# Order of the attention steps in batches 2 to 7 of a fused attention and MoE kernel: k'v ahead of q's second half, one product of x per drawing

## The chip, the core and the metric

The kernel runs on one core of a Trainium2 chip. The metric is the device time of one execution in microseconds (us), the median of several runs. The core has five engines that run beside each other and wait for each other through semaphores: TensorE (PE, with its weight loads as PEld), VectorE (DVE), ScalarE (ACT), GpSimd (POOL) and SyncE (SP), which issues nearly all DMAs here.

## What is computed

The reference is a linear attention followed by a gated feed-forward layer, called the MoE here:

```python
q_s = exp(q - max(q, axis=-1)); q_s = q_s / (sum(q_s, axis=-1) + 1e-9)
k_s = exp(k - max(k, axis=2));  k_s = k_s / (sum(k_s, axis=2) + 1e-9)
kv = einsum('bhsd,bhse->bhde', k_s, v)
x = einsum('bhsd,bhde->bhse', q_s, kv)   # 8 batches, 8 heads, 576 rows, 64 wide
x = x.transpose(0, 2, 1, 3).reshape(4608, 512)
h = x @ w_in                              # 512 x 2048
g = h * erf(softplus(h))
out = g @ w_out                           # 2048 x 512
```

## The kernel before, in words

**The MoE** sets the main rhythm. Two batches make a pair of 1152 tokens, a pair makes 3 blocks of 384 tokens, and each block is worked on in 4 steps of 512 hidden columns, so there are 48 MoE steps, n = 0 to 47. Values are held as two fp16 halves, and each product is made of three fp16 matmuls (high by high, high by low, low by high). Step n consists of `mm1` (line 975, the products pX, pY and pZ of line 999 in a Strassen-like scheme of seven products, copied to H by DVE and ACT in lines 1011 to 1026), softplus (T) and erf (G) on ACT through the helper `act` (line 344), the product with h (U, line 1079), the split into halves (I and O, lines 1093 and 1097) and `mm2` (line 1103), whose products o are those of line 1125. The loop at line 1224 emits, for each n: U of n-1, then four parts of mm1 of n, with I and O of n-1 and three parts of mm2 of n-2 between them, then T and G of n. In the steps with n % 4 == 2 it also splits the next block of x (`finish`, line 369, lines 297, 298 and 388).

**The attention** of batch 0 is in an order written out by hand, batch 1 uses `attention` (line 730), and batches 2 to 7 use `attention16` (line 649), which the change rewrites. Each is a generator. A step of it emits some instructions and yields a share, a number for how much of the pacing it uses up. The steps of one batch are:

- kmax (line 492): the running maximum of k over its rows, on DVE. Its two tiles and kvf below share the two buffers of one tag.
- kT (line 504): the transposes of that maximum on PE into a bank, and the reduction km on DVE. kB (line 517): the result spread back over all rows by PE. ksub (line 662): k minus the maximum, on DVE.
- q_sub (line 451): q minus its row maximum, for each half of the heads and, in odd batches, for the tails of both batches of the pair (qt).
- exps (line 673) on ACT, in a fixed order with the softplus and erf of the MoE.
- kv_mm (line 528): k'v for one half of the heads, 40 matmuls of line 542, and kv_norm (line 554): the division by the sum (rd, its reciprocal, kvf, lines 561 to 565) on DVE.
- q_norm (line 459) and q_halves (line 636) for one half: the division of q by its sum, the fp16 halves (ACT line 640, DVE line 641) written over k's tile, and a transposing DMA on SP (line 643) back into q's tile. So q_halves of a half must come behind k'v of that half.
- kv_max (line 576): mx, the largest value of kvf. kv_split (line 584): a transpose of mx on PE (all_max, line 125, tile x_bk), a chain of small DVE operations (lines 127 to 141) that makes a power of two, and the two halves kvbd of k'v (lines 595 and 596).
- x_mm (line 626): in odd batches xt first (the tails), then x for the four columns c of 128. Each x needs kvbd and the transposed q of its half, and is copied by ACT (x_put, line 443). Behind the second and the fourth, `load_q` issues the next batch's q, and load_kv (line 471) issues k, the tail and the first half of v.

**The order of the work.** `pace` (line 1207) is called three times in each MoE step, behind each part of mm2. A call is a drawing: it draws steps of the attention generator until their summed share reaches a goal that grows with n. A step that yields 0 ends the drawing. Between n = 8 and 16 (less a lead of 2) the shares of one pair are handed out, afterwards one pair per 12 MoE steps. What a drawing emits is a priority and not yet a place in a queue: the order of each engine's queue is fixed when the kernel is built, by a planner that takes the instructions in order of emission but lets later ones go first while, by its own costs, an earlier one is not ready. On the chip each queue is worked off strictly in order.

Before the change the shares of a batch come from the list SHARES16 (line 49). Kmax takes 2.51, kT 0, and kB with ksub 0.16, the second q_sub 0.09, exps 1.58, each half of k'v with q_norm 2.43, each q_halves 1.3, load_kv and kv_max 0.26, kv_split 0.3, xt 0.78 and each x 0.3.

Of the kernel before, what the change touches and what calls it, by code (L numbers as in the profile page):

```python
# [45 lines left out]
OUTS = [0, 1, 2, 3]  # L46

SHARES = [2.51, 0, 0.16, 0.09, 1.58, 2.43, 1.12, 0.26, 0.29, 0.04, 0.78, 1.12, 0.16]
SHARES16 = [2.51, 0, 0.16, 0.09, 1.58, 2.43, 1.3, 2.43, 1.3, 0.26, 0.3, 0.78, 0.3]
LEAD = 2.0  # L50

EXPMASK = 0x7F800000
# [5 lines left out]
def attn_moe_kernel(  # L58
# [280 lines left out]
    def act(out_, in_, func, chain=True, **kw):  # L339

        with ExitStack() as es:
            if chain and last[0] is not None:
                es.enter_context(tc.issue_after(last[0]))
            i = nc.scalar.activation(out_, in_, func, **kw)  # L344
        if chain:
            last[0] = i.ins
        return i
# [49 lines left out]
    def load_half(src, tag, b, hf):  # L397

        s4 = src[b, hf * 4:hf * 4 + 4, 0:SM, :].rearrange("h (p t) d -> p h t d", t=TM)
        if tag == "v" and b == 0 and hf == 1:  # L400
            t = ch.tile([P, 4, TM, D + 1], F32, tag="G", bufs=2, name=f"v_{b}_{hf}")
            nc.gpsimd.memset(t[:, :, :, D:], 1.0)
        elif tag == "v":
            t = vbuf
        else:
            t = at.tile([P, TM, 4, D], F32, tag=tag, name=f"{tag}_{b}_{hf}")
        eng = nc.sync
        for h in range(4):
            eng.dma_start(t[:, h, :, :D] if tag == "v" else t[:, :, h, :], s4[:, h])  # L409
        return t  # L410
# [34 lines left out]
    def hd(t):  # L445
        return t.rearrange("p h d -> p (h d)")
# [45 lines left out]
    def k_max(b, ks, kt):  # L492

        kmax = at.tile([P, H, D], F32, tag="qT", name=f"kmax_{b}")
        k2 = at.tile([P, 2, 4, D], F32, tag="qT", name=f"k2_{b}")
        for hf in range(2):
            nc.vector.tensor_tensor(k2, ks[hf][:, 0:2], ks[hf][:, 2:4], op=ALU.max)
            nc.vector.tensor_tensor(
                kmax[:, hf * 4:hf * 4 + 4, :], k2[:, 0], k2[:, 1], op=ALU.max
            )  # L500
        nc.vector.tensor_tensor(kmax[kt[1]], kmax[kt[1]], kt[0], op=ALU.max)
        return kmax

    def k_max_T(b, kmax):
        bk = bank(f"kT_{b}")
        km2 = hd(kmax)
        for c in range(NC4):
            nc.tensor.transpose(
                bk[:, c * P:(c + 1) * P], km2[:, c * P:(c + 1) * P], ident
            )  # L510
        km = at.tile([P, NC4], F32, tag="km", bufs=1, name=f"km_{b}")
        nc.vector.tensor_reduce(
            km, bk.rearrange("p (c s) -> p c s", c=NC4), axis=AX.X, op=ALU.max
        )
        return km
# [12 lines left out]
    def kv_mm(b, hf):  # L528


        d, kt_ = bat[b], bat[b - b % 2]["kt"]
        bk = bank(f"kv_{b}_{hf}")
        for c in range(2):
            for t in range(TM + 1):
                for a in range(2):
                    h = 2 * c + a
                    if t < TM:
                        kk, vv = d["k"][hf][:, t, h, :], d["v"][hf][:, h, t, :]
                    else:

                        kk, vv = kt_[:, 4 * hf + h, :], vtail[:, 4 * hf + h, :]
                    nc.tensor.matmul(  # L542
                        bk[a * D:(a + 1) * D, c * W:(c + 1) * W], kk, vv,
                        start=(t == 0), stop=(t == TM),
                    )
        return bk
# [7 lines left out]
    def kv_norm(b, hf, bk):  # L554
        if b >= E32:
            if hf == 0:
                bat[b]["kvf"] = at.tile([P, NC4, D], F32, tag="qT", name=f"kvf_{b}")
            kvf = bat[b]["kvf"]
        bkv = bk[:, :2 * W].rearrange("p (c w) -> p c w", c=2)
        rd = at.tile([P, 2, 1], F32, tag="rd", bufs=1, name=f"rd_{b}_{hf}")  # L560
        nc.vector.tensor_scalar_add(rd, bkv[:, :, D:], 1e-9)
        nc.vector.reciprocal(rd, rd)
        cs = slice(2 * hf, 2 * hf + 2)
        if b >= E32:
            nc.vector.tensor_tensor(
                kvf[:, cs, :], bkv[:, :, :D], rd.to_broadcast([P, 2, D]), op=ALU.mult
            )
            return
        for a in range(2):
            ps = slice(a * D, (a + 1) * D)  # L570
            nc.vector.tensor_tensor(
                kv32[b][ps, cs, ps], bkv[ps, :, :D], rd[ps].to_broadcast([D, 2, D]),
                op=ALU.mult,
            )
# [58 lines left out]
                out_, kvbd[b % 2][:, wl, c, :], qT[:, ql], start=(i == 0), stop=(i == 2)  # L633
            )

    def q_halves(src, place, name):

        n = src.shape[1]
        st_ = place.bitcast(F16).rearrange("p (i n) -> p i n", i=2)
        nc.scalar.copy(st_[:, 0], src)  # L640
        nc.vector.tensor_tensor(st_[:, 1], src, st_[:, 0], op=ALU.subtract)
        qT = src.bitcast(F16).rearrange("p (a s) -> p a s", s=P)
        nc.sync.dma_start_transpose(qT, place.bitcast(F16))
        return qT.rearrange("p (i a) s -> p i a s", i=2)

    def flat3(t):
        return t.rearrange("p a b c -> p (a b c)")

    def attention16(b):
        d, j, p = bat[b], b % 2, b // 2  # L650
        even = bat[b - j]
        tl = slice(j * TAIL, (j + 1) * TAIL)
        ks, qs, kt = d["k"], d["q"], even["kt"][tl]
        sh = iter(SHARES16)
        kmax = k_max(b, ks, (kt, tl))
        yield next(sh)
        km = k_max_T(b, kmax)
        q_sub(rows(qs[0]), 16, f"q_{b}_0")
        yield next(sh)
        kb = k_max_rows(b, km)  # L660
        for hf in range(2):
            nc.vector.tensor_tensor(
                ks[hf], ks[hf],
                kb[:, None, hf * 4:hf * 4 + 4, :].to_broadcast([P, TM, 4, D]),
                op=ALU.subtract,
            )
        nc.vector.tensor_tensor(kt, kt, kb[tl], op=ALU.subtract)
        yield next(sh)
        q_sub(rows(qs[1]), 16, f"q_{b}_1")
        if j == 1:  # L670
            q_sub(even["qt"], H, f"qt_{p}")
        yield next(sh)
        for t in (*ks, kt, qs[0], qs[1], *([even["qt"]] if j == 1 else [])):
            act(t, t, AF.Exp, chain=b > 1)
        yield next(sh)
        qT = {}
        for hf in range(2):
            kv_norm(b, hf, kv_mm(b, hf))
            if hf == 0:
                d["v"].append(load_half(v, "v", b, 1))  # L680
            q_norm(rows(qs[hf]), 16, f"q_{b}_{hf}", b)
            yield next(sh)
            qT[hf] = q_halves(flat3(qs[hf]), flat3(ks[hf]), f"{b}_{hf}")
            yield next(sh)
        if j == 1:
            q_norm(even["qt"], H, f"qt_{p}", b)
            qT[2] = q_halves(hd(even["qt"]), hd(even["kt"]), f"{p}_t")
        if b + 1 < B:
            load_kv(b + 1)
        mx = kv_max(b)  # L690
        yield next(sh)
        kv_split(b, mx)
        yield next(sh)
        for i in ((3 * p + 1, 3 * p + 2) if j else (3 * p, 3 * p + 1)):
            while not x_free(i):
                yield 0
        w = next(sh)
        if j == 1:
            bk = bank(f"xt_{p}")
            x = xblock(p * NBK + 1)  # L700
            bk3 = bk.rearrange("p (c s) -> p c s", c=NC4)
            for a in range(2):
                for c in range(NC4):
                    cs = slice(a * TAIL, (a + 1) * TAIL)
                    x_mm(2 * p + a, c, bk3[:, c, cs], qT[2][:, :, c, cs])
            x_put(bk3, x[:, :, SM - T:SM - T + P], None)
            if b + 1 < B:
                bat[b + 1]["qt"] = load_tail(q, "qt", p + 1)
            yield w
        w = next(sh)  # L710
        for c in range(NC4):
            hf, c2 = divmod(c, 2)
            bk = bank(f"x_{b}_{c}")
            q4 = qT[hf].rearrange("p i (t c) s -> p i t c s", c=2)[:, :, :, c2]
            x_mm(b, c, bk.rearrange("p (t s) -> p t s", t=TM), q4)
            x_split(b, c, bk)
            if c2 == 1 and b + 1 < B:
                load_q(b + 1, hf)
            if c == NC4 - 1:
                d["xdone"] = True  # L720
            yield w

    def x_split(b, c, bk, part=None):
        for blk, off, o, w in xcols(b, 0 if b % 2 == 0 else SM + 2 * TAIL, SM)[part or slice(9)]:
# [476 lines left out]
                assert tok("A"), i  # L1201

    w_odd = sum(SHARES[:11]) + NC4 * sum(SHARES[11:])
    per_pair = 2 * (sum(SHARES16[:11]) + NC4 * SHARES16[12]) + SHARES16[11]
    n1 = NG + 4

    def pace(at_n):
# [68 lines left out]
```

## Time and profile before

| | us |
|---|---|
| three runs | 851.73, 853.64, 853.0 |
| median | 853.0 |
| the profiled execution, its own time | 853.86 |
| its span, first to last instruction | 851.7 |
| PE busy in the span | 811.2 |
| DVE busy | 638.2 |
| ACT busy | 503.0 |

The span is what the trace covers; 2.2 us of the profiled execution lie around it. Busy times are of single engines and overlap. In the rows of the profile a line such as "L632 PE x" is line 632 of the kernel, on engine PE, writing tile x; "a <- b" in a list of waits is that a stood still until b had ended. PEld is the loading of weights, which runs beside the matmuls.

### The profile page before, as it was taken

How to read it: one execution, taken by the hardware profiler on the slowest of the kernel's cores; microseconds unless marked ns; L12 is line 12 of the kernel's file. 1: busy time of each engine (PE TensorE's matmuls, PEld its weight loads, DVE VectorE, ACT ScalarE, POOL GpSimd, SP SyncE). 2: the span in 40 equal slices, each digit the busy share in tenths (PEclk: the TensorE clock that was granted, in tenths of full speed). 3: DMA queues.
4: the chain of work that ended last, by engine and by line, in shares of the span. 5: the costliest groups of instructions: out<-in, count | busy, mean ns of one | idle time of the engine just before them, and what ended most of it. 6: DMA issues, size and time to landing. Idle time of an engine off the chain costs nothing.

```text
span 851.7 us, 15370 instructions
## 1 busy us (share of the span) xinstructions
PE 811.2 (95%) x6448; PEld 553.8 (65%) x6448; DVE 638.2 (75%) x913; ACT 503.0 (59%) x633; POOL 17.6 (2%) x37
## 2 busy tenths in 40 slices
PE   2999998899999999999999999999999999999997
PEld 1655557567667667766776676766776676777673
DVE  5999899998997879758865779748866657554543
ACT  2598486777564556555673566555663565543532
POOL 2010000000000000000000000000000000000000
PEclk8899999899999999999999999999999999999999
DMA  9997420016416402412134302322121000100100
GB/s 255 407 250 197 120 75 13 1 25 112 106 35 131 108 9 61 103 31 51 51 70 98 87 14 51 93 51 51 38 51 38 38 2 1 38 1 1 38 1 37
DMA packets 145508, 62.59 MB, mean 73 GB/s; under 512 B 134688, under 2 KB 136736, under 8 KB 145440
## 3 DMA queue, kind: packets, MB, share of 16 engines
q1 hardware_dynamic: 143264, 53.23, 25.1%
q0 software_dynamic: 2176, 8.39, 2.8%
q8 instruction: 50, 0.82, 0.4%
q14 instruction: 18, 0.15, 0.1%
HBM read 45.09 MB, written 9.44 MB: 64 GB/s over the span
## 4 chain that ended last, share of the span: by engine, by line
PE 64%; DVE 19%; ACT 10%; issue 3%; SPq 2%; DMA 1%; ACTq 0%; POOL 0%; DVEq 0%
PE o L1125 27%; PE pX L999 15%; PE pZ L999 7%; ACT G L344 4%; PE o L1116 4%; ACT L344 3%; PE pY L999 3%; DVE G L1079 3%; PE kv L542 2%; DVE H L1097 2%; PE pX L1038 2%; DVE H L1093 2%; SPq L409 2%; PE x L632 1%; DVE wi L298 1%
## 5 line engine op out<-in xcount | busy, mean ns | idle before, releaser
L1125 PE MATMUL o<-wo,H 128*128 128x512 f16 x1584 | 367.0, 380 | 2.8 <-DVE H L1093 1.8
L999 PEld LDWEIGHTS <-wi 128*128 128x128 f16 x3696 | 311.2, 98 | 44.3 <-issue 15.7
L1125 PEld LDWEIGHTS <-H 128*128 128x128 f16 x1584 | 152.7, 98 | 157.4 <-DVE H L1093 2.6
L999 PE MATMUL pX<-x,wi 128*128 128x192 f16 x2112 | 206.2, 248 | 7.6 <-ACT H L1018 4.5
L344 ACT ACT_TABLE_LOAD x104 | 133.4, 1283 | 2.8 <-DVE H L1024 0.8
L1079 DVE SCALAR_TENSOR_TENSOR G<-G,small,H 128x1536 f32<-128x1536 f32 x44 | 79.9, 1817 | 56.2 <-ACT G L344 56.0
L1026 ACT COPY H<-pX 128x384 f32<-128x384 f32 x44 | 20.9, 475 | 165.3 <-PE pX L999 159.9
L999 PE MATMUL pZ<-x,wi 128*128 128x192 f16 x1056 | 104.0, 247 | 3.4 <-ACT x L297 1.8
L344 ACT ACTIVATE G<-H,U 128x768 f32<-128x768 f32 (+1 forms) x60 | 72.7, 1231 | 22.1 <-DVE H L1024 21.5
L1097 DVE TENSOR_TENSOR H<-G,H 128x1536 f16<-128x1536 f32 x44 | 77.2, 1755 | 1.0
L344 ACT ACTIVATE G<-G 128x1536 f32<-128x1536 f32 x48 | 71.2, 1484 | 0.5
L999 PE MATMUL pY<-x,wi 128*128 128x192 f16 x528 | 51.9, 247 | 0.0
L1024 DVE TENSOR_TENSOR H<-pZ,H 128x384 f32<-128x384 f32 x44 | 24.4, 554 | 32.5 <-PE pZ L999 32.1
L1011 DVE COPY H<-pY 128x384 f32<-128x384 f32 x44 | 24.3, 553 | 30.3 <-PE pY L999 30.3
L1116 PE MATMUL o<-wo,G 128*128 128x512 f32 x96 | 43.4, 597 | 0.0
L1093 DVE CAST H<-G 128x1536 f16<-128x1536 f32 x44 | 42.1, 957 | 0.8
L297 ACT ACTIVATE x<-x 128x768 f16<-128x768 f32 (+1 forms) x44 | 32.9, 763 | 12.8 <-DVE x L388 11.1
L1141 DVE TENSOR_SCALAR ob<-o,V 128x512 f32<-128x512 f32 x29 | 21.7, 748 | 24.5 <-PE o L1125 24.5
L298 DVE SCALAR_TENSOR_TENSOR x<-x,x 128x768 f16<-128x768 f32 (+1 forms) x44 | 37.0, 851 | 3.2 <-ACT x L297 3.2
L1013 DVE TENSOR_TENSOR H<-pX,H 128x384 f32<-128x384 f32 x44 | 24.4, 554 | 15.9 <-PE pX L999 15.7
L443 ACT ACTIVATE x<-x 128x384 f32<-128x384 f32 (+1 forms) x52 | 17.5, 394 | 30.0 <-PE x L632 27.4
L1116 PEld LDWEIGHTS o<-wo,G 128*128 128x128 f32 x96 | 17.5, 190 | 18.7 <-issue 18.2
(184 smaller groups left out, 762.7 us busy)
## 6 DMA issues: line engine op xcount, KB each, us to landing
out_dram<-ob SPq DMA_DIRECT2D x32, 256.0 KB, 2.4
vbuf<-in_v_dram SPq DMA_DIRECT2D x60, 128.0 KB, 3.1
q<-in_q_dram SPq DMA_DIRECT2D x56, 128.0 KB, 3.4
k<-in_k_dram SPq DMA_DIRECT2D x56, 128.0 KB, 3.1
wo<-in_moe_w_in_dram SPq DMA_DIRECT2D x4, 1024.0 KB, 17.2
wi<-in_moe_w_out_dram POOLq DMA_DIRECT2D x2, 1024.0 KB, 8.9
wi<-in_moe_w_in_dram SPq DMA_DIRECT2D x2, 1024.0 KB, 9.4
raw<-in_moe_w_out_dram POOLq DMA_DIRECT2D x2, 1024.0 KB, 8.0
```

The costliest lines, as they stand in the source:

```text
L297: nc.scalar.activation(hi, src, AF.Copy, scale=s)
L298: nc.vector.scalar_tensor_tensor(lo, src, s, hi, op0=ALU.mult, op1=ALU.subtract)
L344: i = nc.scalar.activation(out_, in_, func, **kw)
L999: nc.tensor.matmul(o, w[wl][:, c, a * P:(a + 1) * P], x[:, xl, xi, c, :], start=(new and a == 0 and c == 0 and i == 0), stop=(c == 1 and i ...
L1011: nc.vector.tensor_copy(C[0, 0], bank2("Y"))
L1013: add(C[0, 0], bank2("X"), C[0, 0], op=ALU.add)
L1024: add(C[0, 1], bank2("Z"), C[0, 1], op=ALU.add)
L1079: nc.vector.scalar_tensor_tensor(flat(s["G"]), flat(s["G"]), (GB if n in OUT32 else GA)[:, g:g + 1], flat(s["H"]), op0=ALU.mult, op1=ALU.mult,
L1093: nc.vector.tensor_copy(flat(s["gh"]), flat(s["G"]))
L1097: nc.vector.tensor_tensor(flat(s["gl"]), flat(s["G"]), flat(s["gh"]), op=ALU.subtract)
L1116: nc.tensor.matmul(o, s["G"][:, a, ts_], w[:, a, :], start=(first_ and a == 0), stop=(last_ and a == FG - 1),)
L1125: nc.tensor.matmul(o, s[gt][:, a, ts_], w[wl][:, a, :], start=(first_ and a == 0 and i == 0), stop=(last_ and a == FG - 1 and i == 2),)
```

## The change

In `attention16` the steps of one batch get another order, and another share each:

1. kT is emitted in the step of kmax, no longer in that of the first q_sub. It yields 1.8.
2. Both q_sub steps and the step of kB and ksub yield 0.9, exps 1.5.
3. The first half of k'v is a step of its own (0.4), then q_norm (0.75) and q_halves (0.75) of the first half.
4. The second half of k'v and kv_max come next, in one step (0.6), and then kv_split (0.4), all of it ahead of q_norm and q_halves of the second half (0.75 each). Before, kv_max and kv_split came behind them.
5. load_kv comes behind the second q_halves, as before, now in a step with the tails' q_norm and q_halves that yields 0.75 in odd batches and 0 in even ones.
6. xt yields 0.75, and each x yields 0.75 instead of 0.3.

The sum for a pair goes from 27.9 to 28.3. No instruction is added or taken away. `chain=b > 1` is true for all batches that come here, so its removal changes nothing, nor does that of the name given to q_halves.

```diff
-SHARES16 = [2.51, 0, 0.16, 0.09, 1.58, 2.43, 1.3, 2.43, 1.3, 0.26, 0.3, 0.78, 0.3]
+SHARE16 = 1.8 + 0.9 * 3 + 1.5 + 0.4 + 0.75 * 4 + 0.6 + 0.4 + 0.75 * 4
...
-        kmax = k_max(b, ks, (kt, tl))
-        yield next(sh)
-        km = k_max_T(b, kmax)
+        km = k_max_T(b, k_max(b, ks, (kt, tl)))
+        yield 1.8
         q_sub(rows(qs[0]), 16, f"q_{b}_0")
-        yield next(sh)
+        yield 0.9
         kb = k_max_rows(b, km)
...
-        for hf in range(2):
-            kv_norm(b, hf, kv_mm(b, hf))
-            if hf == 0:
-                d["v"].append(load_half(v, "v", b, 1))
+
+        def q_half(hf):
             q_norm(rows(qs[hf]), 16, f"q_{b}_{hf}", b)
-            yield next(sh)
-            qT[hf] = q_halves(flat3(qs[hf]), flat3(ks[hf]), f"{b}_{hf}")
-            yield next(sh)
+            yield 0.75
+            qT[hf] = q_halves(flat3(qs[hf]), flat3(ks[hf]))
+            yield 0.75
+
+        kv_norm(b, 0, kv_mm(b, 0))
+        d["v"].append(load_half(v, "v", b, 1))
+        yield 0.4
+        yield from q_half(0)
+        kv_norm(b, 1, kv_mm(b, 1))
+        mx = kv_max(b)
+        yield 0.6
+        kv_split(b, mx)
+        yield 0.4
+        yield from q_half(1)
         if j == 1:
             q_norm(even["qt"], H, f"qt_{p}", b)
-            qT[2] = q_halves(hd(even["qt"]), hd(even["kt"]), f"{p}_t")
+            qT[2] = q_halves(hd(even["qt"]), hd(even["kt"]))
         if b + 1 < B:
             load_kv(b + 1)
-        mx = kv_max(b)
-        yield next(sh)
-        kv_split(b, mx)
-        yield next(sh)
+        yield 0.75 if j == 1 else 0
...
-            yield w
-        w = next(sh)
+            yield 0.75
         for c in range(NC4):
...
-            yield w
+            yield 0.75
...
-    per_pair = 2 * (sum(SHARES16[:11]) + NC4 * SHARES16[12]) + SHARES16[11]
+    per_pair = 2 * SHARE16 + 0.75 * 2
```

More of the change, by code (lines that the diff above doesn't have):

```diff
@@ L634, in x_mm, with q_halves @@
             )
-    def q_halves(src, place, name):
+    def q_halves(src, place):
         n = src.shape[1]
@@ L653, in attention16 @@
         ks, qs, kt = d["k"], d["q"], even["kt"][tl]
-        sh = iter(SHARES16)
-        kmax = k_max(b, ks, (kt, tl))
-        yield next(sh)
-        km = k_max_T(b, kmax)
+        km = k_max_T(b, k_max(b, ks, (kt, tl)))
+        yield 1.8
         q_sub(rows(qs[0]), 16, f"q_{b}_0")
-        yield next(sh)
+        yield 0.9
         kb = k_max_rows(b, km)
@@ L667, in attention16 @@
         nc.vector.tensor_tensor(kt, kt, kb[tl], op=ALU.subtract)
-        yield next(sh)
+        yield 0.9
         q_sub(rows(qs[1]), 16, f"q_{b}_1")
@@ L671, in attention16 @@
             q_sub(even["qt"], H, f"qt_{p}")
-        yield next(sh)
+        yield 0.9
         for t in (*ks, kt, qs[0], qs[1], *([even["qt"]] if j == 1 else [])):
-            act(t, t, AF.Exp, chain=b > 1)
-        yield next(sh)
+            act(t, t, AF.Exp)
+        yield 1.5
         qT = {}
-        for hf in range(2):
-            kv_norm(b, hf, kv_mm(b, hf))
-            if hf == 0:
-                d["v"].append(load_half(v, "v", b, 1))
+        def q_half(hf):
             q_norm(rows(qs[hf]), 16, f"q_{b}_{hf}", b)
-            yield next(sh)
-            qT[hf] = q_halves(flat3(qs[hf]), flat3(ks[hf]), f"{b}_{hf}")
-            yield next(sh)
+            yield 0.75
[11 more added lines that the diff above has]
+        yield from q_half(1)
         if j == 1:
             q_norm(even["qt"], H, f"qt_{p}", b)
-            qT[2] = q_halves(hd(even["qt"]), hd(even["kt"]), f"{p}_t")
+            qT[2] = q_halves(hd(even["qt"]), hd(even["kt"]))
         if b + 1 < B:
             load_kv(b + 1)
-        mx = kv_max(b)
-        yield next(sh)
-        kv_split(b, mx)
-        yield next(sh)
+        yield 0.75 if j == 1 else 0
         for i in ((3 * p + 1, 3 * p + 2) if j else (3 * p, 3 * p + 1)):
@@ L708, in attention16 @@
                 bat[b + 1]["qt"] = load_tail(q, "qt", p + 1)
-            yield w
-        w = next(sh)
+            yield 0.75
         for c in range(NC4):
```

## The prediction

> **What bounds the kernel now.** I read the page first, then busy time by stage, then the waits of PE, then the timeline around those waits. From the page:
>
> ```profile
> span 851.7 us, 15370 instructions
> PE 811.2 (95%) x6448; PEld 553.8 (65%) x6448; DVE 638.2 (75%) x913; ACT 503.0 (59%) x633; POOL 17.6 (2%) x37
> ...
> PE 64%; DVE 19%; ACT 10%; issue 3%; SPq 2%; DMA 1%; ACTq 0%; POOL 0%; DVEq 0%
> ```
>
> PE is busy 95% of the span, and the chain that ended last runs through it for 64%. The stages show where its idle time lies (columns: PE, PEld, DVE, ACT, POOL, then granted clock, DMA share, GB/s):
>
> ```profile
> 148.00:156.00 8.00, 3.37 (x21) 2.33 (x19) 7.95 (x10) 6.29 (x7) 0.00 (x0) 0.76 0.00 0
> 190.00:690.00 500.00, 492.04 (x4295) 346.04 (x4294) 383.34 (x568) 296.74 (x356) 3.16 (x10) 1.00 0.28 63
> 690.00:852.00 162.00, 155.41 (x1208) 105.59 (x1205) 81.89 (x88) 73.42 (x79) 0.00 (x0) 1.00 0.04 16
> ```
>
> Up to about 190 us the weights are decoded and split, and DVE is full (7.95 of 8.00 in the first row). From 190 to 690 us, where batches 2 to 7 are worked on beside the MoE, PE is busy 492.04 of 500.00: 8.0 us is all that any reordering can give there through visible idle time. After 690 us no attention is left, and the change has nothing to move. The waits of PE in the middle stage say what the 8.0 us are (total, times, longest):
>
> ```profile
> PE xt L632 <- DVE kvbd L595: 2.5, 3, 0.9
> PE pX L999 <- ACT H L1026: 1.3, 2, 0.6
> PE x L632 <- issue: 0.9, 1, 0.9
> PE pX L999 <- DVE H L1021: 0.9, 1, 0.9
> PE x L632 <- DVE kvbd L595: 0.7, 2, 0.4
> PE x L632 <- DVE kvbd L596: 0.6, 3, 0.2
> PE pX L999 <- ACT H L1018: 0.3, 1, 0.3
> ```
>
> Four of the seven rows are the same thing: the products x and xt (L632) stand in PE's queue and their operand kvbd, the split k'v that kv_split writes on DVE, is not there. They add up to 2.5 + 0.9 + 0.7 + 0.6 = 4.7 us in 9 waits. The other three are MoE products of bank pX, 1.3 + 0.9 + 0.3 = 2.5 us.
>
> A wait in this list is shorter than what it costs. In batch 2:
>
> ```profile
> 215.10 0.27 PE L125 MATMUL x_bk<-ident,mx 128*128 128x128 f32 x1
> 215.21 1.15 PE L999 MATMUL pX<-x,wi 128*128 128x192 f16 x12
> 216.20 2.75 PE L1125 MATMUL o<-wo,H 128*128 128x512 f16 x12
> 219.86 0.81 PE L632 MATMUL x<-q,kvbd 128*128 128x512 f16 x3 [0.91 <-issue]
> ```
>
> The 12 products pX last 1.15 us here, yet the next group starts 216.20 - 215.21 = 0.99 us after them: 0.16 us of each group's modelled end lies under its successor. When PE waits, this 0.16 is lost too. So the 9 waits cost 4.7 + 9 x 0.16 = 6.1 us. (The 0.91 put down to issue here is the same kvbd wait.)
>
> [...]
>
> **The change, part by part.** No instruction is added or removed. What moves is the step in which each is emitted. Pacing hands out one third of an MoE step per drawing, and a pair of batches is spread over 36 drawings (12 MoE steps by 3), so one drawing gives 27.9 / 36 = 0.775 of share before and 28.3 / 36 = 0.786 after. Counting the shares through the loop gives, for batch 4 (written MoE step.drawing), kT 15.0, kB 15.1, exps 15.1, kv1 17.1, kv_split 19.0, x0 19.0, x1 and x2 19.1, x3 19.2 before, and kT 13.2, kB 15.0, exps 15.2, kv1 17.1, kv_split 17.1, x0 and x1 18.2, x2 19.0, x3 19.1 after. For batch 5: kv1 23.0, kv_split 25.0, xt 25.0 before; kv1 23.0, kv_split 23.0, xt 24.1 after. A drawing in time: kv_split's transpose for batches 4 and 6, one pair apart, starts at 377.93 and 571.50 us, so (571.50 - 377.93) / 36 = 5.4 us.
>
> ```profile
> 377.93 0.27 PE L125 MATMUL x_bk<-ident,mx 128*128 128x128 f32 x1
> 378.24 0.29 DVE L127 TENSOR_REDUCE x_e<-x_bk 128x1 f32<-128x128 f32 x1 [2.14 <-PE x_bk L125]
> 379.34 0.72 DVE L595 TENSOR_SCALAR kvbd<-kvf,x_s 64x256 f16<-64x256 f32 x2
> 380.12 0.61 PE L632 MATMUL x<-q,kvbd 128*128 128x512 f16 x2 [0.35 <-DVE kvbd L595]
> 383.20 0.48 DVE L596 SCALAR_TENSOR_TENSOR kvbd<-kvf,x_s,kvbd 64x256 f16<-64x256 f32 x1
> 383.75 0.39 PE L632 MATMUL x<-q,kvbd 128*128 128x512 f16 x1 [0.23 <-DVE kvbd L596]
> ...
> 571.50 0.27 PE L125 MATMUL x_bk<-ident,mx 128*128 128x128 f32 x1
> ```
>
> *The waits that go.* Before, kv_split and x0 (or xt) come out of one drawing, so the transpose, a chain of 9 DVE operations up to kvbd's upper half (378.24 to 380.06) and x stand close together; kvbd's lower half ends only at 383.68 and holds x a second time. After, kv_split is emitted 4 drawings before x or xt in batches 4 to 7, 4 x 5.4 = 21.6 us, against the 5.8 us that the chain took from 377.93 to 383.68. In the faster paced batches 2 and 3 it is two drawings or more. All 9 waits should go: -6.1 us.
>
> *The wait that may come.* kv1, kv_max and kv_split are now emitted together, so the transpose x_bk (L125) has to wait for rd, its reciprocal, kvf and mx on DVE. In PE's queue the whole MoE stands behind it. Batch 4 before shows this chain without its transpose:
>
> ```profile
> 352.87 0.29 PE L542 MATMUL kv<-vtail,kt 128*64 128x65 f32 x4
> 354.09 2.75 PE L1125 MATMUL o<-wo,H 128*128 128x512 f16 x12
> 354.56 0.15 DVE L561 TENSOR_SCALAR rd<-kv 128x2 f32<-128x2 f32 x1
> 356.60 0.42 DVE L578 TENSOR_REDUCE mx<-kvf 128x1 f32<-128x256 f32 x1
> ```
>
> From the end of kv at 353.16 to the end of mx at 357.02 pass 3.9 us. The order of each engine's queue is fixed when the kernel is built, by a planner that places an instruction where its own clock has it ready, so PE has other work first, as the o group here, and the wait is the planner's error on the chain. Its error on the 9 DVE operations before x was 0.35 + 0.16 = 0.51 us in batch 4 and 0.91 + 0.16 = 1.07 us in batch 2, so for 4 operations 4/9 of that: 0.23 to 0.48, and I take the middle, 0.35 us. Six batches: +2.1 us. Ends: 0, and 3.9 - 2.0 = 1.9 each (two pX-sized groups ahead of it, 2 x 0.99), or 11.4 us.
>
> *kT beside kmax.* kT's transposes now leave in kmax's drawing and could wait for it. But kmax needs both buffers that it shares with kvf, and kv_split, which releases kvf, is now ahead of it by the whole of x. I take 0. The nearest row bounds it at one last operation of kmax in each of six batches, 6 x 0.69 = 4.1 us:
>
> ```profile
> L501 DVE TENSOR_TENSOR kmax<-kmax,kt x8: 673/687/690, 8.2 to 581.1; 64x512 f32<-64x512 f32 x8
> ```
>
> *xt of batch 3.* There the pace is faster, and kv1, the tail's halves and xt lie within two drawings (12.0 to 12.2). The halves need a transposing DMA between them:
>
> ```profile
> 263.88 0.29 PE L542 MATMUL kv<-vtail,kt 128*64 128x65 f32 x4
> 271.01 1.28 SPq L643 DMA_TRANSPOSE qt<-kt  x1
> qt<-kt SPq DMA_TRANSPOSE x3, 3.1
> ```
>
> The transpose was issued at 271.01 and lands 3.1 later, 274.1, which is 9.9 us after kv1's end at 264.17; two drawings are 10.8 in the later pace and less here. I take 0, since before no wait of PE on such a DMA is listed, and keep up to 2.5 us.
>
> *What else is moved.* On SP the v half, the two transposes and load_kv keep their order among themselves; load_kv of batch 5 leaves in 18.1 instead of 19.0, which is early, and q's reload after x1 and x3 is spread. On POOL the clearing of kvbd (batches 2 and 3) now stands ahead of load_vtail's memsets instead of behind; those wait for PE anyway and hold nobody. On ACT the exps leave two drawings after kB in batches 4 to 7, where they left in kB's own, so ACT finds k already subtracted:
>
> ```profile
> ACT k L344 <- DVE k L662: 13.3, 3, 6.9
> ```
>
> These 13.3 us are ACT's idle time, not PE's, and shorten the way to softplus. I count 0, with the 2.5 us of pX waits as the most that a freer ACT and DVE could give, or as much again lost.
>
> *The early stage.* Batch 2's first steps (kT, kB) come one or two drawings sooner while DVE is full. The row of 148 to 156 us prices what can go wrong: PE was busy 3.37 of 8.00 at a granted clock of 0.76, so a second hole of that kind costs 4.6 us, and losing this one gives as much. MoE work on ACT ends that hole, which the change leaves where it is; I take 0.
>
> **The sum** against the profiled execution, 853.86 us with a span of 851.7: -6.1 + 2.1 = -4.0, giving 849.9. The median of the three runs is 853.0, 0.9 below the profiled one, so the forecast for it is 853.0 - 4.0 = 849.0 us. Its own range: from 846.9 (no new wait) to 851.3.
>
> **The rivals.** *Given back:* the waits only change places. The planner puts each instruction at its own estimate, so x_bk, now the tight one, gets the 6.1 us that x had. For it speak the 29% of the chain that lie on DVE and ACT; against it, that x_bk hangs on 4 operations and not 9, and that the MoE waits, where a gain would be eaten, are 2.5 us in all. Time: 853.0. [...]
>
> *Slower through x_bk:* the transpose stands too early in PE's queue, with less than an o group ahead of it, and DVE's chain of 3.9 us runs behind a long MoE operation. It decides from (6.1 + 1.7) / 6 = 1.3 us a batch; with 1.9 us a batch the time is 853.0 - 6.1 + 11.4 = 858.3. For it: in batch 4 rd itself came 1.4 us after kv (354.56 against 353.16). Against it: the planner knows the DVE queue and let PE run 12 products of pX and 12 of o past such chains.
>
> *More than forecast:* x_bk never waits and the pX waits go as well, since DVE's and ACT's bursts are spread: 853.0 - 6.1 - 2.5 = 844.4.
>
> **How the numbers follow.** Chances: forecast 0.50, given back 0.20, slower 0.18, more 0.12. About 0.2%, 1.7 us, is what a measurement here can tell from no change. The forecast and the last case lie below 851.3, given back within 851.3 to 854.7, slower above: 0.62, 0.20, 0.18. The range goes from 844.4 to 856.0: it takes in the forecast, the given-back case and the near half of the slower one, with the bounds on kT, xt and the early stage falling inside.
>
> **What would show it.** Right: from 190 to 690 us no row of PE on kvbd is left, x_bk starts some 20 us ahead of its x or xt, a wait of PE at x_bk on mx of a few tenths appears, and PE's idle time there falls from 8.0 to about 4 to 5 us. Wrong: long waits at x_bk or kT, xt of batch 3 held by the transposing DMA, PE rows on kvbd still there, or new pX waits on ACT or DVE that eat the gain; a changed hole before 190 us would mean that the start decided.

## The result, and the profile after

The changed kernel takes 867.1 us (median of 6 runs, 861.5 to 870.7), the kernel before 852.5 us beside it. It is slower by 14.6 us by the medians, where 849.0 was forecast and 856.0 was the end of the range. The ratio, taken over all runs, is 1.016 with a 95% interval of 1.012 to 1.020, or 13.6 us. The profiled execution took 870.7 us, the slowest of the six, so its span lies 16.9 us above that of the kernel before and overstates the loss a little.

The page after:

```profile
span 868.6 us, 15364 instructions
PE 819.3 (94%) x6448; PEld 562.5 (65%) x6448; DVE 640.7 (74%) x913; ACT 502.9 (58%) x633; POOL 17.6 (2%) x37
...
PE 65%; DVE 18%; ACT 6%; DMA 4%; issue 3%; SPq 3%; POOL 0%; ACTq 0%; DVEq 0%
```

The matmuls are as many as before (6448), yet PE is busy 8.1 us longer, and DMA, which held 1% of the chain, holds 4%. The stages after, the first of them the whole stretch of batches 2 to 7, the others around one wait (columns as in the prediction: PE, PEld, DVE, ACT, POOL, granted clock, DMA share, GB/s):

```profile
190.00:707.00 517.00, 500.73 (x4345) 355.65 (x4345) 388.36 (x571) 299.87 (x361) 3.16 (x10) 0.98 0.27 62
363.00:369.00 6.00, 3.12 (x21) 1.56 (x18) 5.90 (x10) 0.39 (x1) 0.40 (x2) 1.00 0.42 112
369.00:375.00 6.00, 5.84 (x49) 5.54 (x50) 4.67 (x17) 1.77 (x3) 0.00 (x0) 0.72 0.85 194
375.00:381.00 6.00, 6.00 (x46) 3.89 (x44) 2.92 (x4) 5.36 (x6) 0.00 (x0) 1.00 0.33 70
```

PE is idle 517.00 - 500.73 = 16.3 us there, against 8.0 before; and its granted clock, 1.00 before in every six microseconds of this stage, falls to 0.72 from 369 to 375 us, behind the wait of 3.04 us at x_bk. The waits of PE from 190 to 710 us:

```profile
PE x_bk L125 <- DVE mx L578: 7.5, 4, 3.4
PE xt L632 <- DMA qt<-kt: 2.8, 1, 2.8
PE pX L1001 <- DVE H L1023: 2.7, 1, 2.7
PE kv L542 <- DMA vbuf<-in_v_dram: 0.8, 1, 0.8
PE pX L1001 <- DVE H L1015: 0.8, 1, 0.8
PE kv L542 <- issue: 0.8, 1, 0.8
PE pX L1001 <- ACT H L1020: 0.7, 1, 0.7
```

All rows of PE on kvbd are gone, as forecast. In their place stand x_bk on mx (the transpose in kv_split: two waits of over 3 us, in batches 4 and 6, and two of about 0.5, in batches 5 and 7), xt on the transposing DMA, and pX on DVE. Where the time is lost is read best from the starts of the MoE steps, that is of the first pY product of a step in the timeline:

| MoE step | before, us | after, us | after is late by | |
|---|---|---|---|---|
| 4 | 128.65 | 130.23 | 1.6 | the start, ahead of the change's first step |
| 8 | 188.58 | 187.47 | -1.1 | batch 2 |
| 12 | 258.11 | 268.27 | 10.2 | batches 2 and 3 |
| 16 | 327.03 | 335.91 | 8.9 | |
| 17 | 341.73 | 352.03 | 10.3 | |
| 19 | 373.36 | 389.16 | 15.8 | x_bk of batch 4 |
| 28 | 520.60 | 531.91 | 11.3 | x of batches 4 and 5 no longer wait (1.9 of these 4.5 us in run 4) |
| 29 | 535.30 | 548.03 | 12.7 | |
| 31 | 566.93 | 586.71 | 19.8 | x_bk of batch 6 |
| 38 | 682.22 | 699.18 | 17.0 | end of the attention |

So there are two losses: about 9 us by step 12, and two jumps of 5.5 and 7.1 us at x_bk of batches 4 and 6. The timeline around the first jump:

```profile
357.89 0.64 SPq L409 DMA_DIRECT2D k<-in_k_dram  x1
360.83 0.69 DVE L497 TENSOR_TENSOR k<-k 128x512 f32<-128x512 f32 x1 [3.27 <-DMA k<-in_k_dram]
361.44 1.81 DVE L1081 SCALAR_TENSOR_TENSOR G<-G,small,H 128x1536 f32<-128x1536 f32 x1
362.36 0.29 PE L542 MATMUL kv<-vtail,kt 128*64 128x65 f32 x4
363.58 2.54 PE L1127 MATMUL o<-wo,H 128*128 128x512 f16 x11
364.31 1.76 DVE L1099 TENSOR_TENSOR H<-G,H 128x1536 f16<-128x1536 f32 x1
366.64 0.15 DVE L561 TENSOR_SCALAR rd<-kv 128x2 f32<-128x2 f32 x1
368.69 0.42 DVE L578 TENSOR_REDUCE mx<-kvf 128x1 f32<-128x256 f32 x1
369.16 0.32 PE L125 MATMUL x_bk<-ident,mx 128*128 128x128 f32 x1 [3.04 <-DVE mx L578]
369.54 1.70 PE L1001 MATMUL pZ<-x,wi 128*128 128x192 f16 x12
371.03 2.13 PE L1001 MATMUL pX<-x,wi 128*128 128x192 f16 x12
```

Read from the bottom: x_bk waits 3.04 us for mx. Mx is late because rd, the first of its chain, starts only at 366.64, 4.0 us after k'v. It stands in DVE's queue behind the MoE's long operations, and these are late because DVE stood still for 3.27 us in front of L497: the first of them, L1081, has its input from ACT at 358.58 and starts only behind L497, at 361.44. L497 is the first operation of kmax of the next batch, batch 5, and waits for that batch's k, whose last piece was issued at 357.89. Behind x_bk the 12 products of pZ and of pX take 1.70 and 2.13 us, where 1.15 is usual.

Before, L497 of batch 5 stood 6.8 us behind the start of k's load and did not wait:

```profile
337.89 2.58 SPq L409 DMA_DIRECT2D k<-in_k_dram  x4
344.68 0.68 DVE L497 TENSOR_TENSOR k<-k 128x512 f32<-128x512 f32 x1
```

After, the transposing DMA that frees k's first tile and this load are directly in front of k'v's second half:

```profile
351.64 2.87 SPq L643 DMA_TRANSPOSE q<-k  x1
355.94 2.59 SPq L409 DMA_DIRECT2D k<-in_k_dram  x4
```

The load starts at 355.94, L497 at 360.83, 4.9 us behind it, and k'v's second half at 361.26. Measured from the start of MoE step 16, the load leaves 10.9 us behind it before (337.89 against 327.03) and 20.0 us behind it after (355.94 against 335.91).

### The profile page after: what moved, and what is told of

Its sections match the earlier page's. It is cut to its first block, busy times and chain, and to the rows that moved or that the text cites. A ratio compares the mean times of both kernels' runs of the same rounds, so it can differ in the third digit from the quotient of the medians.

```text
span 868.6 us, 15364 instructions
## 1 busy us (share of the span) xinstructions
PE 819.3 (94%) x6448; PEld 562.5 (65%) x6448; DVE 640.7 (74%) x913; ACT 502.9 (58%) x633; POOL 17.6 (2%) x37
## 4 chain that ended last, share of the span: by engine, by line
PE 65%; DVE 18%; ACT 6%; DMA 4%; issue 3%; SPq 3%; POOL 0%; ACTq 0%; DVEq 0%
PE o L1127 27%; PE pX L1001 15%; PE pZ L1001 7%; PE o L1118 3%; PE pY L1001 3%; ACT G L344 3%; DVE G L1081 3%; SPq L409 2%; ACT L344 2%; PE kv L542 2%; PE pX L1040 2%; DVE H L1099 2%; PE x L632 2%; DMA q<-k 2%; DVE x L298 1%
## 5 line engine op out<-in xcount | busy, mean ns | idle before, releaser
L1001 PEld LDWEIGHTS <-wi 128*128 128x128 f16 x3696 | 318.0, 100 | 45.1 <-issue 18.0
L1001 PE MATMUL pX<-x,wi 128*128 128x192 f16 x2112 | 210.0, 251 | 9.3 <-ACT H L1020 4.9
L344 ACT ACT_TABLE_LOAD x104 | 133.4, 1283 | 10.9 <-DVE H L1026 9.1
L1081 DVE SCALAR_TENSOR_TENSOR G<-G,small,H 128x1536 f32<-128x1536 f32 x44 | 79.9, 1816 | 50.6 <-ACT G L344 50.5
## 6 DMA issues: line engine op xcount, KB each, us to landing
wo<-in_moe_w_in_dram SPq DMA_DIRECT2D x4, 1024.0 KB, 16.9
```

What stands on the lines that cost most here:

```text
L1001: nc.tensor.matmul(o, w[wl][:, c, a * P:(a + 1) * P], x[:, xl, xi, c, :], start=(new and a == 0 and c == 0 and i == 0), stop=(c == 1 and i ...
L1081: nc.vector.scalar_tensor_tensor(flat(s["G"]), flat(s["G"]), (GB if n in OUT32 else GA)[:, g:g + 1], flat(s["H"]), op0=ALU.mult, op1=ALU.mult,
```

## The experiments

Ratios are to the kernel before, run beside each group of experiments; its median was 852.0 beside the first four, 852.2 beside the next four and 853.5 beside the last three. Gains in us are differences of medians; by the ratios, those of runs 2 and 3 are 8.0 and 7.5 us.

**1. kv_split one step later.**

```diff
-        kv_split(b, mx)
-        yield 0.4
-        yield from q_half(1)
+        second = q_half(1)
+        yield next(second)
+        kv_split(b, mx)
+        yield 0.4
+        yield from second
```

> The changed kernel with one step moved: kv_split is emitted one step later, behind q_norm of the second half, so that its transpose x_bk stands a drawing behind kv_max in PE's queue; all else as changed. Theory A, the loss is mainly PE standing at x_bk for mx (7.5 us in 4 waits in the changed profile) and the slow clock behind the two long ones: the MoE steps 17 to 19 and 29 to 31 lose 5.5 and 7.0 us against before, which should go, so about 867 - 12.5 = 854.5 us, no PE row of x_bk on mx over 0.3 us, and run to run spread back to about 3 us. Theory B, the loss is made in the early stage, batches 2 and 3 (the changed kernel is 10.2 us behind at step 12): then 865 us or more stays.

866.0 us, ratio 1.016 (1.013 to 1.019): nothing gained.

```profile
PE x_bk L125 <- DVE mx L578: 7.9, 4, 3.6
```

Taken as written, theory A failed and B held. But the row of PE's waits says that the wait to be removed was still there, so the run did not test its cost. The 0.6 share of k'v's step is less than a drawing (0.786): q_norm left in the same drawing, kv_split in the next, and x_bk stood behind 12 products o instead of 11. One step was no distance.

**2. kmax held behind kv_split.** The queue of DVE is changed, not the place of kv_split:

```diff
-        km = k_max_T(b, k_max(b, ks, (kt, tl)))
+        with ExitStack() as es:
+            if b > 2:
+                es.enter_context(tc.issue_after(bat[b - 1]["split"]))
+            kmax = k_max(b, ks, (kt, tl))
+        km = k_max_T(b, kmax)
```

(`split` is the last DVE operation that kv_split emits, line 601 of the kernel before. `tc.issue_after` makes kmax wait for it in the order of the queue.)

> The changed kernel with kmax of batches 3 to 7 put behind kv_split of the batch before in DVE's queue; kv_split stays directly behind k'v's second half. Theory A1, mx is late because DVE, ahead of it, stands 3.3 and 3.7 us at kmax's first operation (L497) for the next batch's k by DMA: then DVE's waits at L497 (20.8 us in 9) fall under 6 us, x_bk's waits in batches 4 and 6 fall from 3.2 and 3.6 to under 0.7 us, and the time is about 855 us. Theory A2, x_bk is simply too near to k'v and kmax has nothing to do with it: the waits at x_bk stay over 2 us and the time over 863.

857.9 us, ratio 1.0065 (1.004 to 1.009), 9.2 us less than the changed kernel. Waits of PE:

```profile
PE xt L633 <- DMA qt<-kt: 3.8, 1, 3.8
PE pX L1006 <- DVE H L1028: 2.7, 1, 2.7
PE x_bk L125 <- DVE mx L578: 1.8, 4, 0.5
```

The longest wait at x_bk is 0.5 us. DVE still stands 12.3 us at L497 in 5 waits, more than the 6 expected, but behind kv_split, where PE does not depend on it. In batch 4 DVE's queue now goes from ob straight to the MoE's G:

```profile
357.90 0.75 DVE L1148 TENSOR_SCALAR ob<-o,V 128x512 f32<-128x512 f32 x1 [2.03 <-PE o L1132]
359.71 1.82 DVE L1086 SCALAR_TENSOR_TENSOR G<-G,small,H 128x1536 f32<-128x1536 f32 x1 [1.06 <-ACT G L344]
```

G starts 1.8 us behind ob, where the changed kernel needed 4.6 (356.80 to 361.44). This shows that DVE's wait for k made mx late; theory A2 falls.

**3. The new order from batch 4 on.** Batches 2 and 3 keep the old order and its pace:

```diff
-            yield from attention(b) if b < E32 else attention16(b)
+            yield from attention(b) if b < E32 else attention16_old(b) if b < 4 else attention16(b)
```

> The new order for batches 4 to 7 only; batches 2 and 3 keep the old order and shares. Theory B, early stage: the 8.9 us that the changed kernel is behind at step 16 go, less about 2 that it is behind at step 4 already by other causes, so about 860 us. Theory A alone (the early stage's difference is noise of the start): 866 us. The waits at x_bk of batches 4 and 6 stay in both, at 3 us.

858.3 us, ratio 1.007 (1.005 to 1.009), 8.8 us less than the changed kernel. x_bk still waits 7.6 us in 4. So batches 2 and 3 hold the other half of the loss. (`attention16_old` is the function of the kernel before; the pacing of that pair, not shown here, is the old one too.)

**4. The kernel before with kv_split earlier.**

```diff
             yield next(sh)
+            if hf == 1:
+                kv_split(b, kv_max(b))
             qT[hf] = q_halves(flat3(qs[hf]), flat3(ks[hf]), f"{b}_{hf}")
...
-        mx = kv_max(b)
-        yield next(sh)
-        kv_split(b, mx)
+        yield next(sh)
         yield next(sh)
```

> The kernel before with one edit: kv_max and kv_split are emitted ahead of q_halves of the second half instead of behind load_kv; all shares and all other steps as before. If the prediction's first term holds by itself (the 9 waits of x and xt on kvbd, 6.1 us, go once kv_split is earlier, and x_bk, a step of 2.43 behind k'v, does not wait): about 846.5 us, no PE row on kvbd. If every shift of an attention step disturbs the planner's order by as much as it helps: 852 us or more, with new PE rows elsewhere.

848.1 us, ratio 0.995 (0.993 to 0.997): faster than both. Waits of PE from 190 to 690 us:

```profile
PE pX L999 <- ACT H L1026: 1.3, 2, 0.6
PE x L632 <- issue: 1.1, 1, 1.1
PE pX L999 <- DVE H L1021: 1.0, 2, 0.6
PE kB L521 <- DVE km L512: 0.6, 1, 0.6
PE pX L999 <- DVE H L1013: 0.4, 1, 0.4
PE pX L999 <- ACT H L1018: 0.4, 1, 0.4
```

Of the nine waits for kvbd one of 1.1 us is left (batch 2), and x_bk has no row. The idea of the change is worth about 4 us by itself.

**5. Both repairs**, those of runs 2 and 3 together.

> Both repairs at once: new order for batches 4 to 7 only, and kmax of a batch held behind kv_split of the batch before. If the two losses are separate, they add: 867.1 - 9.2 (hold) - 8.8 (batches 2 and 3 old) = 849.1 us, 3 us ahead of before, with the gain that the prediction's first term gives to batches 4 to 7 left over (six of the nine kvbd waits). If they are two sides of one loss (one DVE that runs late from the start on), about 857 us remains.

850.0 us, ratio 0.9964 (0.995 to 0.998). The two losses are separate and add, within 1 us: 867.1 - 9.2 - 8.8 = 849.1 was expected.

**6. As run 5, with the new order in batch 3 too** (`b < 3` for `b < 4`).

> As the one before, but batch 3 has the new order too and only batch 2 the old. Says which of the two batches makes the early loss. Theory B3: it is batch 3 (subtraction of k in front of pX on DVE 2.8 us, the tail's transposing DMA in front of xt 2.9 to 4.0 us, each with slow clock behind it): then about 849 + 7 = 856 us and a PE wait of xt on the DMA of about 3 us. Theory B2: it is batch 2 (k'v waits for the exps and for v, 2.8 us): then about 851 us and no wait of xt on the DMA over 1 us.

852.6 us, ratio 1.0003 (0.999 to 1.002), between the two theories. Waits of PE from 125 us on:

```profile
PE pX L1081 <- DVE H L1103: 2.6, 3, 1.3
...
PE xt L634 <- DMA qt<-kt: 1.6, 1, 1.6
```

Batch 3 costs 852.6 - 850.0 = 2.6 us, batch 2 on top of it 857.9 - 852.6 = 5.3 us (run 2 against this one). They are not independent: with batch 2 in the old order, batch 3's longest wait at pX is 1.3 us and that at xt 1.6, where run 2 has 2.7 and 3.8.

**7. The old order with the new spacing of x.**

```diff
-SHARES16 = [2.51, 0, 0.16, 0.09, 1.58, 2.43, 1.3, 2.43, 1.3, 0.26, 0.3, 0.78, 0.3]
+SHARES16 = [2.11, 0, 0.16, 0.09, 1.48, 2.03, 1.0, 2.03, 1.0, 0.26, 0.4, 0.78, 0.75]
```

> The kernel before, its order of steps unchanged, but each x yields 0.75, so that it has a drawing of its own; the 1.8 a batch that this takes are taken from the long shares ahead of it, so a batch's sum stays 13.56. Tests the second half of the change alone. If the spacing of x has a worth of its own: below 850 us. If the x waits on kvbd are all there is (x0 still comes in kv_split's drawing or the next one): some of the nine waits go, 849 to 852 us. If earlier steps by themselves bring long waits: over 855 us.

854.3 us, ratio 1.002 (1.001 to 1.004). A drawing for each x brings nothing by itself here, where the shares ahead of it are shortened to make room. x and xt still stand right behind kv_split, and eight waits for kvbd are left, 5.2 us in all. One of them, 1.48 us at xt (273.28 us), has products of 2.12 and 1.47 us instead of 1.15 behind it; that the 2 us lost are these was not tested. None of the three expected cases was met exactly.

**8. kv_split two steps later**, behind q_halves of the second half:

```diff
-        kv_split(b, mx)
-        yield 0.4
         yield from q_half(1)
+        kv_split(b, mx)
+        yield 0.4
```

> The changed kernel with kv_split emitted behind q_halves of the second half (two steps later than changed, one later than in the first run of this study); kmax not held, so DVE still waits for k's DMA in front of mx. Theory: x_bk only needs to stand further from k'v than DVE's delay of 3 to 4 us; then its waits in batches 4 and 6 go (under 0.7 us), x and xt still find kvbd ready, and the time is about 858 us as with the hold. If the late DVE itself costs the time and not its distance to x_bk: 864 us or more.

859.8 us, ratio 1.007 (1.005 to 1.010). No wait at x_bk is listed any more, although DVE still waits 16.9 us for k. It comes within 2 us of run 2 by the other road: either the chain is on time, or its reader stands further off. In batches 4 and 6 the late DVE now holds pX, for 1.6 us each, in place of x_bk's 3.0 and 3.4. The row, counted from 125 us on, holds these two and three waits of the early stage, the longest of which, 2.7 us, the changed kernel has as well:

```profile
PE pX L1001 <- DVE H L1023: 8.3, 5, 2.7
```

**9 and 10. Filling a wait with useless work.** Both kernels have the new order from batch 4 on and kv_split one step later; the second adds 24 matmuls into x_bk's bank in batches 4 and 6, ahead of the transpose that overwrites them.

```diff
+        z = ident.bitcast(F16)
+        for _ in range(24 if name in ("x4", "x6") else 0):
+            nc.tensor.matmul(bk[:, :256], z[:, :P], z, start=True, stop=True)
         nc.tensor.transpose(bk[:, :P], mx.to_broadcast([P, P]), ident)
```

> The partner of the next run: new order for batches 4 to 7 only, kv_split one step later, so that in batches 4 and 6 PE's queue has k'v, 12 of pX, 12 of o, then x_bk. The one step later changed nothing before, so about 858.3 us, with two waits at x_bk of about 3.4 us, each with slow clock behind it (1.7 and 2.9 us in the profile of the run from batch 4 on).

> The same with 24 matmuls of 128x256 on the identity ahead of x_bk in batches 4 and 6, written into x_bk's own bank and overwritten: 24 x 0.108 = 2.6 us of work that nobody needs, in the 3.4 us in which PE stands still; the rest of PE's queue is the same. Theory clock: the long wait costs twice, once as a wait and once by the slow clock behind it, and a wait of 0.8 us doesn't lower the clock; PE is late by the same 3.4 us, and the time falls by the second part, 1.7 + 2.9 = 4.6 us, to about 854 us, less where the clock didn't fall in every execution. Rival: the clock has nothing to do with the wait, then the time is the same, 858, or up to 5.2 us more.

857.0 us without the filling, ratio 1.0037 (1.002 to 1.005), and 853.9 us with it, ratio 1.0017 (1.001 to 1.003). Batch 4 without:

```profile
352.27 2.75 PE L1207 MATMUL o<-wo,H 128*128 128x512 f16 x12
358.24 0.47 PE L129 MATMUL x_bk<-ident,mx 128*128 128x128 f32 x1 [3.22 <-DVE mx L582]
358.51 2.13 PE L1081 MATMUL pZ<-x,wi 128*128 128x192 f16 x12
360.43 1.50 PE L1081 MATMUL pX<-x,wi 128*128 128x192 f16 x12
```

and with:

```profile
353.14 2.78 PE L128 MATMUL x_bk<-ident 128*128 128x256 f16 x24
356.45 0.32 PE L129 MATMUL x_bk<-ident,mx 128*128 128x128 f32 x1 [0.53 <-DVE mx L582]
356.61 1.15 PE L1081 MATMUL pZ<-x,wi 128*128 128x192 f16 x12
357.60 1.15 PE L1081 MATMUL pX<-x,wi 128*128 128x192 f16 x12
```

x_bk starts 5.90 us behind the start of the o products with the filling and 5.97 us without, so the wait was filled and not shortened. The 24 added matmuls take 2.78 us. But the products behind x_bk run at their usual 1.15 us, and the granted clock from 356 to 362 us is 1.00 where it was 0.72 without. In the two profiles, steps 17 to 19 are shorter by 1.5 us and steps 29 to 31 by 2.0. The gain of the runs is 1.7 us by the ratios and 3.1 by the medians, against 4.6 expected. The two intervals just overlap, so its size stays open; that 2.6 us of added work cost 2.6 us each time, the rival's other end, is excluded.

**11. Run 4 with kmax held as in run 2.**

> The kernel before with kv_split ahead of q_halves of the second half, as in the fourth run, and kmax held behind kv_split of the batch before. If DVE's waits for k's DMA (7.3 us in 4 in the fourth run) cost PE anything there: about 846.5 us. If they are idle time that nobody needs: 848 us, the same as the fourth run.

848.0 us, ratio 0.9939 (0.9925 to 0.995), against 0.9948 in run 4: the same, although DVE's wait for k fell from 7.3 us in 4 to 1.2 us in 1. So that wait cost nothing here, where nothing near behind it is needed by PE.

## Why the prediction was wrong

**The waits that go** (-6.1 us): right, and a little large. All nine are gone in the changed kernel. Run 4, which does this and little else, gained about 4 us: one wait of 1.1 us stayed, one of 0.6 came (kB on km), and PE's idle time from 190 to 690 us fell from 8.0 to 4.8 us.

**The wait that may come** (+2.1 us): this step failed. It said that "the wait is the planner's error on the chain" and scaled that error with the number of DVE operations, 0.35 us a batch. For batches 5 and 7 that was near: 0.5 us, and batches 2 and 3 have no such wait. In batches 4 and 6 it was over 3 us, because the error did not arise in the chain at all: DVE was standing at an operation of another step (L497) for a DMA that landed later than the queue's order supposed, and L1081 behind it, ready at 358.58, did not start before 361.44. The prediction looked for what the chain needs, and not for what stands ahead of it on its engine and what that waits for. The row was there to be asked for: before, DVE already waited 5.2 us in 3 cases at L497 for k. Run 2 shows this cause. Two readings had hidden it. The part on what else is moved said of load_kv that it leaves earlier, "which is early". In the trace k's load leaves later, 20.0 instead of 10.9 us behind step 16, because it needs the tile that the transposing DMA of the first q_halves frees. Counted as the prediction counts, that q_halves goes from 16.2 to 17.0, directly ahead of k'v's second half in 17.1; the prediction's list leaves it out. The other reading is that of kmax's buffers, below.

**The price of a wait** was mis-sized too. The jumps at steps 17 to 19 and 29 to 31 are 5.5 and 7.1 us, the waits 3.0 and 3.4. In run 2, without the long waits, each of these stretches takes 32.85 us, still 1.2 more than before; so the late x_bk cost 37.13 - 32.85 = 4.3 us in batch 4 and 38.68 - 32.85 = 5.8 us in batch 6. What goes beyond the wait is the lowered clock behind it (0.72 in batch 4, with products of 1.70 and 2.13 us instead of 1.15, and 0.55 in batch 6), which the prediction priced only for the early stage.

**xt of batch 3**: the place was named and bounded at 2.5 us, the value taken was 0; it was 2.8 us, and 3.8 in run 2.

**The early stage and what else is moved**, taken as 0: batches 2 and 3 cost 8.8 us (run 3). With kmax held they cost 857.9 - 850.0 = 7.9 us, of which 5.3 come with batch 2 being in the new order and 2.6 with batch 3 (runs 2, 5 and 6). Named waits there are xt above, pX on DVE of 2.7 us where the subtraction of k stands ahead of it in DVE's queue, and pX and k'v with 0.7 to 0.8 us each. The waits at k'v are batch 2's (0.67 us for its exps, 0.76 with no releaser shown, 0.81 for v's second half, up to 192.54 us). The clock from 192 to 198 us is 0.72, and from step 7 to step 9 the changed kernel takes 37.8 us where the one before takes 34.1. In run 6, with batch 2 in the old order, none of the three is listed in that stretch, the clock there is 1.00, and the stretch takes 34.0. So this part of the loss is batch 2's k'v reaching PE ahead of its operands. Which move in batch 2 sets it off was not taken apart and stays open. A candidate is that the two halves of k'v are now 1.9 of share apart instead of 3.73, with the load of v's second half between them.

**kT beside kmax**: right in the outcome, no wait of kT in that stage, but not in the reason. The prediction had all of kmax behind kv_split, because of the buffers that it shares with kvf. Its first operation, L497, needs only one of them and stands ahead of kv_split in DVE's queue, in batch 4 at 360.83 against 371.94 for L595, and before at 344.68 against 379.34; only L498 comes behind. So the very operation that held DVE up was taken to be out of the way.

**The rivals.** "Slower through x_bk" named the right place, and its sum for six batches (11.4 us) was near the 12.6 us of the two jumps, but it put an equal wait into each of six batches where two had a long one, so that the sums meet is chance. It had 0.18; with the early stage beside it, the outcome went past its 858.3. "Given back" is not what happened: run 4 shows that the waits, once gone, do shorten the time.

## What to carry to other kernels

Before moving a producer and its reader close together, walk up the producer's own queue: the wait of an operation ahead of it there can become the reader's wait, as here 3.27 us of DVE at L497 for a DMA became 3.04 us of PE at x_bk. A long wait of TensorE can cost more than its length: here waits of 3.0 and 3.4 us came to 4.3 and 5.8. And when an experiment brings nothing, look first whether the wait it was to remove is gone from its profile.

## What the runs showed of the hardware

The granted clock fell behind some waits of PE and not behind others. In the changed kernel these are the stages behind the wait of pX (2.7 us), behind that of xt (2.8), and behind x_bk of batch 6 (3.4):

```profile
250.00:256.00 6.00, 6.00 (x39) 4.52 (x38) 1.38 (x3) 4.56 (x4) 0.00 (x0) 0.72 0.00 0
...
290.00:296.00 6.00, 6.00 (x57) 3.98 (x54) 4.22 (x6) 5.30 (x8) 0.00 (x0) 1.00 0.69 169
...
566.00:572.00 6.00, 6.00 (x42) 5.45 (x40) 4.09 (x15) 1.63 (x2) 0.00 (x0) 0.55 0.87 201
```

As means of six microseconds, behind one wait of 2.8 us it stayed at 1.00, behind one of 2.7 to 0.72, behind one of 3.4 to 0.55. It also fell to 0.72 from 192 to 198 us, behind the three waits of 0.67 to 0.81 us at batch 2's k'v, and in run 7 to 0.86 from 270 to 276 us and to 0.86 from 276 to 282, around a wait of 1.48 us. In the kernel before it stayed at 1.00 from 214 to 226 us, around the wait of 0.91 us at x of batch 2. That it is PE's standing still, and not something else in these stages, run 10 shows for x_bk of batch 4: with the wait filled the clock stayed at 1.00, where run 9 had 0.72. Why waits of about the same length, 2.7 and 2.8 us, fare differently no run here shows. The changed kernel's runs spread over 9 us, with mean clocks from 0.976 (870.7 and 867.8 us) to 0.993 (861.5 us), while the six of the kernel before beside them lie within 2.5 us. The 25 of it beside runs 5 to 8 lie within 5.2, so part of that difference may be the small number of runs.
